# A recurrence followed by a gated feed-forward on one core: one down projection stands at another place, and the last tile is stored differently

## The chip, the cores and the metric

The kernel runs on one core of one Trainium2 chip. The number that counts is device time of one execution in microseconds (us). Before the change it is 585.62 us, the median of three runs (585.18 to 587.04 us).

## The reference

Two stages follow each other. The first is a linear recurrence over 768 steps for 4 batches of 8 heads with 48 channels each; the second takes its output as 3072 tokens of 384 values and applies a gated feed-forward with 1536 inner units.

```python
for t in range(S):
    kt, vt, rt = (k[:, :, t], v[:, :, t], r[:, :, t])
    cur = np.einsum('bhd,bhe->bhde', u[None] * kt, vt)
    y[:, :, t] = np.einsum('bhd,bhde->bhe', rt, state + cur)
    state = w[None, :, :, None] * state + np.einsum('bhd,bhe->bhde', kt, vt)

gate = 1.0 / (1.0 + np.exp(-(x @ w_gate)))
val = x @ w_val
return (gate * val @ w_out).astype(np.float32)
```

## The kernel before

**Tiling.** The 768 steps are cut into 12 chunks of 64. The heads of a chunk form two groups, so there are 24 groups, numbered 0 to 23. Two chunks make a tile of 512 tokens, and the feed-forward works through six tiles (0 to 5) in 12 slices of 128 inner units each.

**One slice of the feed-forward** is: 18 matmuls of 128x512 into two PSUM banks (`up`, L443), a sigmoid on ACT (L452), a product on DVE (L456), a rounding to fp32r on ACT (L461), the remainder on POOL or DVE (L465), and 9 matmuls (`down`, L481) that add to three accumulator banks, acc0 to acc2. Operands are kept as a rounded part and a remainder, and three products are formed of them. The down projection of a slice stands one slice late, so that its inputs are ready. After slice 11 of a tile the three banks are written out by `store` (L490): for each bank ACT copies the left 256 columns (L493), DVE the right 256 (L494), both into one `wf` buffer, of which there are two, and SP issues one DMA of 256 KB to the result.

**One group of the recurrence** is: `scores` (L304; for groups from 8 on it begins with the 32 matmuls that read the state, L284, then 64 matmuls into `sc`, L315), `keep` (L320, two masked copies on DVE, L323), `apply` (32 matmuls `ring<-score,toks`, L284, then in `outer` 32 matmuls `ring<-toks`), `x_high` (ACT, L402) and `x_low` (DVE, L406), which write the next feed-forward tile's input, and `add_state` (DVE, L379), which releases the PSUM bank that the next `up` needs. `prepare` (ACT L259, POOL L265 and L275, DVE L271) readies the next group, and `load` (SP, L101 and L106) fetches one further on.

**What sets the order.** Every engine executes its instructions in the order in which the program records them. The first part (tile 0 with groups 0 to 7) is written out as a table of steps (`START`, L42): the letter names the step and the number its group or slice; `U` is `up`, `g m H q` are the parts after it, `D` is `finish` (a down projection, with the store after the last one), `L X` are loads and `A R k T` are the four parts of `prepare`. From item 13 on (slice 0 of tile 1) a loop (L563) records for each item: `up`, the gate, then for slices 0, 3, 6 and 9 the scores and the masked copies of one group, then the down projection of the item before, then the rest of the group. Items are counted through: 0 to 12 belong to tile 0 (its first slice has two halves), 13 to 24 to tile 1, and so on. In the loop, `finish(i - 1)` is left out for item 13, because the table has already recorded `D.12`.

After the loop there is a branch (L597) around a fallback for unusual decays; it is not taken into the fallback here.

Of the kernel before, what the change touches and what calls it, by code (L numbers as in the profile page):

```python
# [10 lines left out]
F32 = mybir.dt.float32  # L11
# [7 lines left out]
B, H, S, D = 4, 8, 768, 48  # L19
DM, DF = H * D, 1536  # L20
P = 128
# [4 lines left out]
CT = B * C  # L26
# [7 lines left out]
TILES = [[c, c + 1] for c in range(0, NC, 2)]  # L34
# [15 lines left out]
U.4 Tv.6 j.6 Z.6 g.4 ov.5 w.6 D.3 m.4 c.7 o.6 K.6 H.4 U.5 j.7 c.8 g.5 qv.4 w.7 j.8 I.6 O.6 h.6 D.4  # L50
d.6 m.5 w.8 l.6 s.6 F.6 H.5 ov.7 U.6 qv.5 c.9 ov.8 k.7 c.10 Tv.7 j.9 Z.7 g.6 D.5 m.6 U.7 w.9 K.7
H.6 o.9 j.10 g.7 q.6 c.11 I.7 O.7 h.7 D.6 d.7 m.7 l.7 H.7 s.7 F.7 w.10 q.7 j.11 U.8 ov.10 D.7 w.11
g.8 ov.11 U.9 m.8 H.8 q.8 D.8 g.9 m.9 H.9 L.8 X.8 U.10 q.9 D.9 g.10 m.10 H.10 U.11 q.10 D.10 g.11
m.11 H.11 U.12 q.11 A.8 R.8 k.8 T.8 D.11 g.12 m.12 H.12 qv.12 D.12
"""


# [1 line left out]
def rwkv_then_moe(ctx: ExitStack, tc: tile.TileContext, wd, ch, tk, wt, rk0, vn0, wd0, out):  # L59
    nc = tc.nc  # L60
# [3 lines left out]
    hp = ctx.enter_context(tc.tile_pool(name="hp", bufs=2))  # L64
    hq = ctx.enter_context(tc.tile_pool(name="hq", bufs=2))
    wtmp = ctx.enter_context(tc.tile_pool(name="wtmp", bufs=2))
# [136 lines left out]
    W3, WH = 3 * DM, 3 * DM // 2  # L203
# [100 lines left out]
    def scores(n):  # L304
        t, r, k = dec[n], chan[n][:, 0], chan[n][:, 1]
        sc = ga[n] = two_banks()
        if n >= FIRST:
            yb[n] = one_bank(), one_bank()
            from_state(n)
        for kk, rr, at in ((k, t[:, 0], 0), (t[:, 1], r, 256)):  # L310
            for p, p2 in PP:
                o = at + (2 * p + p2) * C
                for be, gm in QUARTERS:
                    row, cs = slice(64 * be, 64 * be + D), (4 * p + 2 * (be ^ gm) + p2) * C
                    nc.tensor.matmul(  # L315
                        sc[64 * gm : 64 * gm + 64, be, o : o + C],
                        kk[row, cs : cs + C], rr[row, cs : cs + C], start=True, stop=True,
                    )

    def keep(n):  # L320
        sc, t = ga.pop(n), score[n % 2]
        for m, at in ((0, 0), (1, 256)):
            nc.vector.copy_predicated(  # L323
                t.rearrange("q (b m i) -> q b m i", b=2, m=4),
                masks[:, m].bitcast(I32).unsqueeze(1).unsqueeze(1).broadcast_to([P, 2, 4, C]),
                sc[:, :, at : at + 256].rearrange("q b (m i) -> q b m i", m=4),
            )

    def apply(n):
        c, g = GROUPS[n]  # L330
        v, t = toks[n][:, 1], score[n % 2]
        if n < FIRST:
            yb[n] = one_bank(), one_bank()
            if c:
                from_state(n)
                nc.tensor.drain()
        for p, p2 in PP:
            for s in range(2):
                for gm in range(2):
                    be, row = gm ^ s, slice(64 * gm, 64 * gm + 64)  # L340
                    m, at = D if s else 64, (4 * p + 2 * be + p2) * D
                    i = (4 * be + 2 * p + p2) * C
                    into_y(
                        n, s, be, m, slice((2 * p + p2) * C, (2 * p + p2 + 1) * C),
                        v[row, at : at + m], t[row, i : i + C], True,
                    )

    def outer(n):
        k, v = toks[n][:, 0], toks[n][:, 1]
        for p, p2 in PP:  # L350
            for be in range(2):
                for gm in range(2):
                    row, at = slice(64 * gm, 64 * gm + 64), (4 * p + 2 * be + p2) * D
                    m, o = D if be else 64, 256 + (2 * p + p2) * D
                    into_y(
                        n, be, gm ^ be, m, slice(o, o + D), k[row, at : at + m],
                        v[row, at : at + D], True,
                    )
# [6 lines left out]
    def decay_state(n):  # L365
        g, st = states(n)
        for p in range(2):
            for s in range(2):
                nc.scalar.activation(  # L369
                    st[:, p, s], st[:, p, s], AF.Copy,  # L370
                    scale=pw[0:112, 4 * g + 2 * p + s, 64:65],
                )

    def add_state(n):
        g, st = states(n)
        for s in range(2):
            y = yb[n][s][0:112, 256 : 256 + 4 * D].rearrange("q (p x) -> q p x", p=2)
            if GROUPS[n][0]:
                nc.vector.tensor_tensor(st[:, :, s], st[:, :, s], y, ALU.add)  # L379
            else:  # L380
                nc.vector.tensor_copy(st[:, :, s], y)
# [18 lines left out]
    def x_high(n):  # L400
        for x, y in x_of(n, 0):
            nc.scalar.copy(out=x, in_=y)  # L402

    def x_low(n):
        for (x, y), (hi, _) in zip(x_of(n, 1), x_of(n, 0)):
            nc.vector.tensor_tensor(x, y, hi, ALU.subtract)  # L406
# [8 lines left out]
    def fills(n):  # L415
        c, g = GROUPS[n]
        ti = TILE_OF[c]
        if ti == 0:
            co = CT * TILES[ti].index(c)
            for j in range(3) if g == 1 else ():  # L420
                fill(xt[ti], j, slice(co, co + CT))
        elif c == TILES[ti][-1]:
            for j in (2,) if g == 1 else (0, 1):
                fill(xt[ti], j, slice(0, 2 * CT))
# [62 lines left out]
    def accumulators():  # L487
        return [pacc.tile([P, 512], F32, name=f"acc{d}") for d in range(3)]

    def store(acc, dst):  # L490
        for d in range(3):
            o = wtmp.tile([P, W3], F32, name="wf")[:, 0:512]
            nc.scalar.copy(out=o[:, 0:CT], in_=acc[d][:, 0:CT])  # L493
            nc.vector.tensor_copy(o[:, CT:], acc[d][:, CT:])  # L494
            nc.sync.dma_start(
                out=out[d * P : (d + 1) * P, dst], in_=o.rearrange("q (c t) -> q c t", t=CT)
            )


    halves = [(0, g) for g in range(HALF)] + [(1, g) for g in range(HALF)] + [(2, g) for g in range(HALF, NF)]  # L500
    items = [(0, h, f) for h, f in halves]
    n0 = len(items)
    for ti in range(1, len(TILES)):
        items += [(ti, 2, f) for f in range(NF)]
    moes, accs = {}, {}

    def moe_of(it):
        ti, h, f = it
        if ti not in accs:
            accs[ti] = accumulators()  # L510
        if (ti, h) not in moes:
            cols = (slice(0, CT), slice(CT, 2 * CT), slice(0, 2 * CT))[h]
            moes[ti, h] = Moe(xt[ti], accs[ti], cols)
        return moes[ti, h]

    def finish(i):
        ti, h, f = items[i]
        moe_of(items[i]).down(f)
        if f == NF - 1:
            store(accs[ti], slice(TILES[ti][0], TILES[ti][-1] + 1))  # L520


    steps = {
# [19 lines left out]
    for step in START.split():  # L543
        name, _, arg = step.partition(".")
# [3 lines left out]
    def prepare(n):  # L548
        if n < len(GROUPS):
            bonus_keys(n)  # L550
            queries(n)
            keys(n)
            if GROUPS[n][0] < NC - 1:
                token_keys(n)

    def load(n):
        if n < len(GROUPS):
            load_channels(n)
            load_tokens(n)
# [3 lines left out]
    for i in range(n0, len(items)):  # L563
        ti, h, f = items[i]
        m = moe_of(items[i])
        m.up(f)
        m.gate(f)
        attend = f in SLOTS and n < 4 * (ti + 2) and n < len(GROUPS)
        if attend:
            scores(n)  # L570
            if GROUPS[n][0] < NC - 1:
                decay_state(n)
            keep(n)
        if i > n0:
            finish(i - 1)
        if attend:
            apply(n)
            if GROUPS[n][0] < NC - 1:
                outer(n)
            x_high(n)  # L580
            x_low(n)
            if GROUPS[n][0] < NC - 1:
                add_state(n)
            prepare(n + 1)
            fills(n)
            load(n + 2)
            n += 1
        if i == n0 + 8:
            range_flag()
    assert n == len(GROUPS)  # L590
    finish(len(items) - 1)


# [3 lines left out]
    with tc.If(bad != 0):  # L597
        with ExitStack() as g:
# [22 lines left out]
            with tc.For_i(0, NC) as c:  # L621
                for p in range(NP):
                    nc.sync.dma_start(
                        out=rkc[:, p].rearrange("q a b i -> q (a b i)"),
                        in_=rk0[bass.ds(c, 1), p].rearrange("o q x -> (o q) x"),
                    )
                with tc.For_i(0, C) as i:
                    for lo, side in ((0, 1), (64, 0)):
# [3 lines left out]
                        for p in range(NP):  # L632
                            nc.sync.dma_start(
                                out=vb[lo : lo + D, p], in_=src[:, p].broadcast_to([D, B, 64])
# [25 lines left out]
                    out=xg[bass.ds(c, 1)].rearrange("o q p t -> (o q) p t"),  # L660
                    in_=yc.rearrange("q p b i -> q p (b i)"),
# [3 lines left out]
            with tc.For_i(0, NC, 2) as c:  # L665
                for j in range(3):
                    for to, lo, n, p in (
# [3 lines left out]
                            out=xr[to : to + n, j],  # L671
                            in_=xg[bass.ds(c, 2), lo : lo + n, p].rearrange("c q t -> q c t"),
# [4 lines left out]
                m = Moe(x, accumulators(), slice(0, 512))  # L677
# [93 lines left out]
```

## Time and profile before

| | before |
|---|---|
| median of the runs | 585.62 us |
| the profiled execution's own time | 585.8 us |
| its span | 584.0 us |
| PE (matmul) busy | 539.5 us, 92% |
| DVE, ACT, POOL busy | 36%, 33%, 25% |

The span is the time from the first to the last instruction of the program on the core; about 1.8 us of the execution's time lie around it. PE is busy for 92% of the span, the other compute engines for about a third, and matmul records overlap a little, because a matmul's record reaches to the end of its pipeline. In a timeline a group of equal instructions on one engine is one row with its start, its length, and in square brackets the idle time before it with what ended it. A suffix q (SPq) is the engine's sequencer, which issues DMAs.

### The profile page before, as it was taken

The page shows a single profiled execution, that of the slowest core. Times are in us where ns is not written, and L with a number is a line of the kernel's source. Part 1 is how long each engine was busy: PE and PEld are TensorE (multiplying, and loading weights), DVE is VectorE, ACT ScalarE, POOL GpSimd, SP SyncE. Part 2 cuts the span into 40 slices and gives each one's busy share as a digit, 9 for nine tenths or more (in the row PEclk, how much of TensorE's full clock was granted, in tenths as well). Part 3 has the DMA queues.
Part 4 walks back from the last instruction along what each step waited for, and adds up shares of the span by engine and source line. Part 5 has one row for each costly group of instructions (what it writes and reads, how often), then busy time and mean ns, then how long its engine had stood idle before and what let it go on. Part 6 is the DMA issues. An engine that isn't in the chain of part 4 may idle for free. (4 is left out here: it accounts for less than half of the span.)

```text
span 584.0 us, 12860 instructions
## 1 busy us (share of the span) xinstructions
PE 539.5 (92%) x5689; PEld 435.8 (75%) x5689; DVE 212.5 (36%) x339; ACT 190.0 (33%) x421; POOL 147.2 (25%) x125
## 2 busy tenths in 40 slices
PE   3755988999899999999999999999999999999994
PEld 2645866788688878788888778878778788888882
DVE  7787999932313313312312313312313212101101
ACT  4365565432323313413313413313413212211221
POOL 3420410322213313313313313313312211211210
PEclk9966998999799999999999999999999999999998
DMA  8489440110600112230012130023130001100001
GB/s 310 176 345 353 153 183 10 33 52 18 231 2 1 15 60 84 62 122 2 9 67 83 59 126 2 7 68 84 57 128 2 9 3 19 55 1 1 0 0 59
DMA packets 13117, 44.54 MB, mean 76 GB/s; under 512 B 2080, under 2 KB 2464, under 8 KB 11648
## 3 DMA queue, kind: packets, MB, share of 16 engines
q1 hardware_dynamic: 13056, 43.66, 21.9%
q8 instruction: 46, 0.75, 0.5%
q14 instruction: 15, 0.12, 0.1%
HBM read 36.58 MB, written 4.72 MB: 71 GB/s over the span
## 5 line engine op out<-in xcount | busy, mean ns | idle before, releaser
L443 PE MATMUL ring<-xt,wx 128*128 128x512 f32 (+1 forms) x1314 | 323.2, 400 | 12.8 <-DVE wf L224 7.2
L443 PEld LDWEIGHTS ring<-xt,wx 128*128 128x128 f32 x1314 | 248.2, 193 | 71.8 <-issue 9.3
L465 POOL TENSOR_TENSOR h<-sg,h 128x512 fp32r<-128x512 f32 x68 | 89.6, 1318 | 363.9 <-ACT h L461 363.9
L481 PE MATMUL acc<-h,wx 128*128 128x512 f32 (+1 forms) x657 | 163.0, 392 | 0.4 <-POOLq L597 0.4
L456 DVE TENSOR_TENSOR sg<-ring,sg 128x512 f32<-128x512 f32 (+1 forms) x73 | 49.9, 684 | 287.9 <-PE ring L443 287.9
L481 PEld LDWEIGHTS acc<-h,wx 128*128 128x128 f32 x657 | 120.5, 188 | 27.7 <-POOLq L597 0.8
L461 ACT CAST h<-sg 128x512 fp32r<-128x512 f32 (+1 forms) x73 | 44.8, 614 | 146.5 <-DVE sg L456 146.5
L452 ACT ACTIVATE sg<-ring 128x512 f32<-128x512 f32 (+1 forms) x73 | 43.2, 592 | 143.6 <-PE ring L443 143.5
L323 DVE COPY_PREDICATED score<-masks,sc 128x512 f32<-128x512 int32 x48 | 36.0, 751 | 14.7 <-PE sc L315 13.9
L265 POOL TENSOR_TENSOR dec<-chan,tabk 128x512 f32<-128x512 f32 x21 | 29.1, 1385 | 20.6 <-DMA chan<-in_ch 12.7
L402 ACT CAST xt<-ring 112x256 fp32r<-112x256 f32 (+1 forms) x52 | 17.2, 375 | 45.5 <-PE ring L284 45.4
L259 ACT ACTIVATE dec<-chan,wu 128x128 f32<-128x128 f32 x96 | 30.7, 399 | 2.9 <-DMA chan<-in_ch 2.9
L406 DVE TENSOR_TENSOR xt<-ring,xt 112x256 fp32r<-112x256 f32 (+1 forms) x52 | 19.9, 419 | 30.2 <-ACT xt L402 28.7
L315 PE MATMUL sc<-dec,chan 48*64 48x64 f32 x768 | 17.4, 232 | 8.5 <-DVE chan L271 7.2
L284 PEld LDWEIGHTS ring<-score,toks 64*48 64x48 f32 (+1 forms) x768 | 15.4, 143 | 12.3 <-issue 6.9
L284 PEld LDWEIGHTS ring<-dec,state 48*48 48x48 f32 (+1 forms) x704 | 13.6, 134 | 13.8 <-issue 8.3
L284 PE MATMUL ring<-score,toks 64*48 64x64 f32 (+1 forms) x768 | 18.8, 242 | 5.4 <-DVE score L323 4.0
L369 ACT ACTIVATE state<-state,pw 112x96 f32<-112x96 f32 x80 | 23.4, 366 | 0.0
L284 PE MATMUL ring<-dec,state 48*48 48x64 f32 (+1 forms) x704 | 17.1, 230 | 6.3 <-ACT sg L452 4.5
L315 PEld LDWEIGHTS sc<-dec,chan 48*64 48x64 f32 x768 | 14.9, 146 | 10.3 <-DVE chan L271 7.2
L275 POOL TENSOR_TENSOR toks<-toks,tabn 128x384 f32<-128x384 f32 x17 | 18.0, 1060 | 9.6 <-ACT tabn L181 8.7
L216 ACT ACTIVATE wf<-wr 128x1152 f32<-128x1152 f32 (+1 forms) x13 | 15.3, 1192 | 15.3 <-DMA wr<-in_wt 10.7
(48 smaller groups left out, 213.9 us busy)
## 6 DMA issues: line engine op xcount, KB each, us to landing
wr<-in_wt SPq DMA_DIRECT2D x11, 1152.0 KB, 8.7
chan<-in_ch SPq DMA_DIRECT2D x24, 512.0 KB, 4.1
toks<-in_tk SPq DMA_DIRECT2D x24, 400.0 KB, 4.7
out_y<-wf SPq DMA_DIRECT2D x18, 256.0 KB, 2.2
xt<-xt SPq DMA_DIRECT2D x30, 64.0 KB, 2.3
wr<-in_wt SPq DMA_DIRECT2D x2, 576.0 KB, 7.2
xt<-xt SPq DMA_DIRECT2D x12, 32.0 KB, 4.8
wu<-in_wd SPq DMA_DIRECT2D x1, 8.0 KB, 1.6
```

What stands on the lines that cost most here:

```text
L259: nc.scalar.activation(t[:, 1, cs], k[:, cs], AF.Copy, scale=wu[:, 1, 4 * g + m : 4 * g + m + 1])
L265: eng.tensor_tensor(v4(t[:, 0]), v4(chan[n][:, 0]), bc2(table_of(n)[:, :, ::-1]), ALU.mult)
L284: nc.tensor.matmul(yb[n][bank][64 * half : 64 * half + m, cs], lhsT, rhs, start=first, stop=stop, skip_group_check=True,)
L315: nc.tensor.matmul(sc[64 * gm : 64 * gm + 64, be, o : o + C], kk[row, cs : cs + C], rr[row, cs : cs + C], start=True, stop=True,)
L323: nc.vector.copy_predicated(t.rearrange("q (b m i) -> q b m i", b=2, m=4), masks[:, m].bitcast(I32).unsqueeze(1).unsqueeze(1).broadcast_to ...
L369: nc.scalar.activation(st[:, p, s], st[:, p, s], AF.Copy, scale=pw[0:112, 4 * g + 2 * p + s, 64:65],)
L443: nc.tensor.matmul(o[:, self.cols], w[a][:, g * DM + kt * P : g * DM + (kt + 1) * P], self.x[:, kt, b, self.cols], start=(k == 0), stop=(k ...
L452: nc.scalar.activation(sg[:, c], self.pair[f][0][:, c], AF.Sigmoid)
L456: nc.vector.tensor_tensor(sg[:, c], self.pair.pop(f)[1][:, c], sg[:, c], ALU.mult)
L461: nc.scalar.copy(out=h[:, 0, c], in_=sg[:, c])
L465: eng.tensor_tensor(h[:, 1, c], self.sg.pop(f)[:, c], h[:, 0, c], ALU.subtract)
L481: nc.tensor.matmul(self.acc[d][:, self.cols], w[a][:, 2 * DM + d * P : 2 * DM + (d + 1) * P], h[:, b, self.cols], start=(f == 0 and k == 0 ...
```

## The change

Two edits in the order and one in the store.

- `D.12`, the last down projection of tile 0 with the store of that tile, leaves the end of the table. The loop now calls `finish(i - 1)` for item 13 too, so it stands behind the scores and masked copies of group 8 and ahead of that group's `apply`.
- `A.8 R.8 k.8 T.8` (the preparation of group 8) stand one slice earlier in the table, ahead of `D.10`.
- The last tile is written out by a new function, `store_last`. Bank 0 is copied whole by ACT and bank 1 whole by DVE, each into a `wf` buffer. Bank 2 is copied in two halves, one by ACT and one by DVE, into two `sg` buffers, and each half has a DMA of its own. So there are four DMAs instead of three, and none of the copies takes a buffer from which an earlier bank is still being sent.

```diff
-g.8 ov.11 U.9 m.8 H.8 q.8 D.8 g.9 m.9 H.9 L.8 X.8 U.10 q.9 D.9 g.10 m.10 H.10 U.11 q.10 D.10 g.11
-m.11 H.11 U.12 q.11 A.8 R.8 k.8 T.8 D.11 g.12 m.12 H.12 qv.12 D.12
+g.8 ov.11 U.9 m.8 H.8 q.8 D.8 g.9 m.9 H.9 L.8 X.8 U.10 q.9 D.9 g.10 m.10 H.10 U.11 q.10 A.8 R.8
+k.8 T.8 D.10 g.11 m.11 H.11 U.12 q.11 D.11 g.12 m.12 H.12 qv.12
...
+    def store_last(acc, c):
+        copies = nc.scalar.copy, nc.vector.tensor_copy
+        for d in range(2):
+            o = wtmp.tile([P, W3], F32, name="wf")[:, 0:512]
+            copies[d](out=o, in_=acc[d])
+            nc.sync.dma_start(
+                out=out[d * P : (d + 1) * P, c : c + 2], in_=o.rearrange("q (c t) -> q c t", t=CT)
+            )
+        for i in range(2):
+            o = hp.tile([P, 512], F32, name="sg")[:, 0:CT]
+            copies[i](out=o, in_=acc[2][:, i * CT : (i + 1) * CT])
+            nc.sync.dma_start(out=out[2 * P : 3 * P, c + i], in_=o)
...
         if f == NF - 1:
-            store(accs[ti], slice(TILES[ti][0], TILES[ti][-1] + 1))
+            if ti == len(TILES) - 1:
+                store_last(accs[ti], TILES[ti][0])
+            else:
+                store(accs[ti], slice(TILES[ti][0], TILES[ti][-1] + 1))
...
-        if i > n0:
-            finish(i - 1)
+        finish(i - 1)
```

On PE, around the start of tile 1, before the change. The accumulators of tile 0 are `acc_416` to `acc_418`; `L315` are the last matmuls of the scores of group 8, and `ring<-score_98,toks` begins its `apply`:

```order
L481 MATMUL acc_416<-h,wx 128x512 x3
L481 MATMUL acc_417<-h,wx 128x512 x3
L481 MATMUL acc_418<-h,wx 128x512 x3
L443 MATMUL ring<-xt,wx 128x512 x18
...
L315 MATMUL sc<-dec,chan 64x64 x16
L315 MATMUL sc<-chan,dec 64x64 x16
L284 MATMUL ring<-score_98,toks 64x64 x2
```

The same place on PE with the change:

```order
L443 MATMUL ring<-xt,wx 128x512 x18
...
L315 MATMUL sc<-dec,chan 64x64 x16
L315 MATMUL sc<-chan,dec 64x64 x16
L481 MATMUL acc_416<-h,wx 128x512 x3
L481 MATMUL acc_417<-h,wx 128x512 x3
L481 MATMUL acc_418<-h,wx 128x512 x3
L284 MATMUL ring<-score_98,toks 64x64 x2
```

The nine matmuls have moved past one `up` and the scores, and now stand between the scores and the `apply` of group 8.

On SP, the DMA issues from the loads of group 8 to those of group 10, before and with the change (minus and plus):

```order
 L101 DMA chan<-in_ch 128x1024
 L106 DMA toks<-in_tk 128x800
-L495 DMA out_y<-wf 128x512 x3
 L101 DMA chan<-in_ch 128x1024
 L106 DMA toks<-in_tk 128x800
+L495 DMA out_y<-wf 128x512 x3
 L101 DMA chan<-in_ch 128x1024
 L106 DMA toks<-in_tk 128x800
```

The loads of group 9 have moved ahead of the three stores of tile 0; those of group 10 still follow them.

On DVE, the copies that `store_last` makes at the end of the program and what each waits for, with the change (`acc_5014` and `acc_5015` are banks 1 and 2 of the last tile; the words in brackets are the engines and DMAs waited for):

```order
L456 TENSOR_TENSOR sg<-ring,sg 128x512 [waits PE_49,Activation_49] x11
L504 COPY wf<-acc_5014 128x512 [waits DMAHW6_49,PE_49]
L510 COPY sg<-acc_5015 128x256 [waits Activation_49,Pool_49]
L612 TENSOR_LOAD flag [waits DVE_49]
L613 COMPARE_AND_BRANCH
```

DVE has two copies there instead of three; the first waits for PE and no longer for ACT, the second waits for ACT.

## Rows read from the trace of the kernel before

**Rows 1.** Page, part 1: busy us, share of the span, instructions.

```profile
PE 539.5 (92%) x5689; PEld 435.8 (75%) x5689; DVE 212.5 (36%) x339; ACT 190.0 (33%) x421; POOL 147.2 (25%) x125
```

**Rows 2.** Timeline of PE, 140 to 164: start, length, what, [idle before, releaser].

```profile
140.63 4.28 PE L481 MATMUL acc<-h,wx 128*128 128x512 f32 x18
144.75 4.36 PE L443 MATMUL ring<-xt,wx 128*128 128x512 f32 x18
149.04 0.68 PE L284 MATMUL ring<-dec,state 48*64 48x64 f32 x32
...
152.29 1.12 PE L284 MATMUL ring<-score,toks 64*64 64x64 f32 x32 [1.64 <-DVE score L323]
...
154.74 0.46 PE L284 MATMUL ring<-toks 64*48 64x48 f32 x9 [0.72 <-issue]
155.13 6.22 PE L443 MATMUL ring<-xt,wx 128*128 128x512 f32 x18
161.19 2.25 PE L481 MATMUL acc<-h,wx 128*128 128x512 f32 x9
```

**Rows 3.** Windows: stretch, its length, busy us (count) of PE, PEld, DVE, ACT, POOL, clock, DMA.

```profile
152.20:159.00 6.80, 5.99 (x73) 4.96 (x74) 2.01 (x6) 1.81 (x6) 2.27 (x2) 0.50 0.81 301
239.40:249.30 9.90, 9.50 (x189) 7.55 (x189) 5.24 (x11) 4.97 (x15) 3.50 (x3) 1.00 0.39 122
```

**Rows 4.** Timeline, 239 to 250: the start of tile 2 on PE and ACT.

```profile
239.48 0.68 PE L284 MATMUL ring<-dec,state 48*64 48x64 f32 x32
...
245.20 0.38 ACT L493 COPY wf<-acc 128x256 f32<-128x256 f32 x1 [2.12 <-DMA out_y<-wf]
...
247.10 2.33 PE L443 MATMUL ring<-xt,wx 128*128 128x512 f32 x9 [0.40 <-DVE state L379]
...
249.27 2.25 PE L481 MATMUL acc<-h,wx 128*128 128x512 f32 x9
```

**Rows 5.** Timeline of PE, 320 to 340: the start of tile 3.

```profile
327.25 0.68 PE L284 MATMUL ring<-dec,state 48*64 48x64 f32 x32
...
337.29 2.21 PE L481 MATMUL acc<-h,wx 128*128 128x512 f32 x9
```

**Rows 6.** Timeline of ACT and SP, 114 to 134.

```profile
114.45 0.53 SPq L101 DMA_DIRECT2D chan<-in_ch  x1
...
132.55 0.60 ACT L452 ACTIVATE sg<-ring 128x512 f32<-128x512 f32 x1 [2.79 <-PE ring L443]
```

**Rows 7.** Windows, columns as in Rows 3: one slice earlier, and where group 8 is prepared.

```profile
129.90:135.90 6.00, 6.00 (x28) 4.86 (x27) 0.69 (x1) 1.11 (x2) 1.24 (x1) 1.00 0.00 0
135.90:140.40 4.50, 4.50 (x21) 3.62 (x20) 0.71 (x1) 1.89 (x6) 3.97 (x3) 1.00 0.00 0
```

**Rows 8.** Timeline, 573 to 579: the last tile's copies and DMA issues.

```profile
574.29 0.37 ACT L493 COPY wf<-acc 128x256 f32<-128x256 f32 x1 [1.95 <-PE acc L481]
574.70 0.42 DVE L494 COPY wf<-acc 128x256 f32<-128x256 f32 x1 [3.01 <-ACT wf L493]
574.98 0.37 ACT L493 COPY wf<-acc 128x256 f32<-128x256 f32 x1 [0.32 <-PE acc L481]
...
575.84 0.90 SPq L495 DMA_DIRECT2D out_y<-wf  x1
...
577.93 0.37 ACT L493 COPY wf<-acc 128x256 f32<-128x256 f32 x1 [2.57 <-PEq L597]
...
578.79 0.33 SPq L495 DMA_DIRECT2D out_y<-wf  x1
```

**Rows 9.** Source line L597, the branch: durations ns min/median/max, first and last start.

```profile
L597 SPq EVENT_SEMAPHORE  x8: 17/17/17, 582.1 to 582.6; - x8
...
L597 SPq COMPARE_BRANCH  x1: 45/45/45, 579.2 to 579.2; - x1
```

**Rows 10.** DMA issues, 148 to 156 and 575 to 577: count, KB, median us to landing.

```profile
chan<-in_ch SPq DMA_DIRECT2D x3, 512.0 KB, 6.6
...
out_y<-wf SPq DMA_DIRECT2D x2, 256.0 KB, 2.6
```

## The prediction

> **What bounds the kernel now.** I read the shares of the page first: PE is busy for 92% of the span [rows 1], so time can be won only where PE stands still or runs slowly, or behind its last matmul. Then the timeline of PE around the two places that the change touches, then the granted clock in windows, and last the timeline and the branch at the end.
>
> At the start of tile 1 the reader is to see a hole. The down projections of items 11 and 12 run back to back from 140.63, `up` of item 13 from 144.75, the state and score matmuls of group 8 from 149.04; then PE waits 1.64 us for the masked copies of DVE and later 0.72 us more, until `up` of item 14 begins at 155.13 and takes until 161.19 [rows 2]. The masked copies cannot begin before the scores end, and nothing stands between the scores and `apply` on PE. Over 152.2 to 159.0 the granted clock is 0.50, the lower of the two levels (1.2 GHz) [rows 3]; before it PE had run the small matmuls of the scores and then stood still. So `up` of item 14 takes 155.13 to 161.19 = 6.06 us, where item 13's takes 144.75 to 149.04 = 4.29.
>
> The starts of tiles 2 and 3 already have the order that tile 1 is to get: scores, down projection with its store, apply. There the whole chain from the state matmuls to the next down projection takes 249.27 - 239.48 = 9.79 us at a clock of 1.00 [rows 3, 4] and 337.29 - 327.25 = 10.04 us [rows 5].
>
> At the end the third bank waits. Banks 0 and 1 are copied from 574.29 and 574.98, but the third copy starts only at 577.93, when the first bank's DMA has landed and its `wf` buffer is free (the view names PE's sequencer there; but PE's last matmul is long done. DVE ends the first bank at 574.70 + 0.42 = 575.12, the issue follows 0.03 later, and the DMAs land 2.6 us after issue: 575.15 + 2.6 = 577.75). Its DMA is issued at 578.79 [rows 8, 10]. SP then branches at 579.2, and its next instruction stands at 582.1 [rows 9], from where a fixed chain leads to the end at 584.0.
>
> **Part 1, the moved down projection.** Its 9 matmuls cost the same, 4.12 / 2 = 2.06 us by the start-to-start of the eighteen [rows 2]. New times: item 11's down ends at 140.63 + 2.06 = 142.69; `up` of item 13 takes 4.29, so the state matmuls of group 8 begin at 146.98; from there the rows of tiles 2 and 3 stand for what comes, 9.79 to 10.04, I take 9.9. The next down projection begins at 156.9 instead of 161.19: **4.3 us won**, 4.15 to 4.4 by the two rows. The two idle times (2.36 us) and the slow `up` (1.77 us) are the larger part of it; the rest is the apply that no longer runs at the lower clock.
>
> What the move adds is in the 9.79 to 10.04 already: the three copies of ACT and DVE now stand ahead of `x_high` and `add_state` of group 8 on those engines, and the third one waits for a landed DMA (2.12 us at tile 2), which shows on PE as 0.40 us before the second half of the next `up` [rows 4, 5]. The input of the moved matmuls is ready well before they now begin, at about 148.5, since before the change they ran from 142.69. On SP the loads of group 9 pass the three stores. They can be issued right behind those of group 8 at 114.45 [rows 6], when group 6, whose buffers they take, is done; so the stores do not run against them, and the preparation of group 9 does not wait for a load. That costs nothing: SP only has to wait for buffers that are free by then, and if they are not, the last rival below is the price.
>
> **Part 2, the preparation of group 8, one slice earlier.** Four ACT, one DVE and two POOL instructions. Where they stand before, ACT is busy for 1.89, DVE 0.71 and POOL 3.97 us in a window of 4.5, other work included; in the 6.0 us one slice earlier they are busy for 1.11, 0.69 and 1.24 [rows 7]. The two together fit into the 6.0 on each engine (3.0, 1.4 and 5.2). ACT has one hole for it, 2.79 us ahead of the sigmoid at 132.55 [rows 6], and gets no more than 1.89. PE is busy throughout both windows. Cost: **0**; the cover is 0.9 us on ACT (2.79 less 1.89), and beyond that the sigmoid would be late by the rest. The loads that it needs are issued from 114.45 on.
>
> **Part 3, the last store.** Bank 0: one ACT copy of 512 columns instead of 256; ACT takes 0.60 us for 512 columns out of PSUM [rows 6]. 574.29 + 0.60 = 574.89, and SP issues at 574.92 (the step from a copy's end to SP's issue is 0.03 us at the third bank: 577.93 + 0.37, 0.04 to DVE, + 0.42 gives 578.76, and SP issues at 578.79). Bank 1: DVE needs 0.69 for 512 columns [rows 7], from 574.98 to 575.67; issue 575.70. Bank 2 is complete 0.69 us after bank 1, the distance of the first two copies, at 575.67. ACT's half takes 0.37, to 576.04; DVE's half waits for ACT's and takes 0.42, from 576.07 to 576.49 [rows 8].
>
> Could the halves run side by side? DVE's copy of a half starts at 574.70, behind the end of ACT's at 574.66 [rows 8]; before the change both also write one buffer, with the change they don't, but DVE's wait for ACT is still listed. The sum takes them one after the other. The Trainium skill, "PSUM — Partial Sum Buffer", section "PSUM bank collisions raise a hardware error", has two engines that read one bank at the same time as an error, so by that rule the split of bank 2 can't earn an overlap; side by side, DVE would be done 0.4 us sooner, of which SP's issues below would let through less than 0.1. The trace agrees with the rule, with 0.04 us between the two.
>
> SP's second issue took 0.90 us, from 575.84 to 576.74, where the last one took 0.33 [rows 8]. I take it that whatever held it until 576.74 is still there, because PE's end has not moved. Then the third issue runs 576.79 to 577.12 and the fourth 577.17 to 577.50, and SP branches at 577.54 instead of 579.16 (578.79 + 0.33 and the same step): **1.6 us won**. If the hold is gone, DVE's half sets the fourth issue, 576.53 to 576.86, and 2.3 us are won. The fourth DMA lands by 577.17 + 2.6 = 579.8, before SP's next instruction at 577.54 + 2.9 = 580.4 (579.2 to 582.1 in [rows 9]), so the landing does not set the end. The other bound: if the end did go by the landing and a half lands no sooner than a whole bank, the win is 578.79 - 577.17 = 1.6 again.
>
> **Sum.** 4.3 + 1.6 = 5.9 us off the profiled execution's 585.8 (span 584.0 and 1.8 around it) gives 579.9; the median of the runs lies 0.2 lower, so **579.7 us**.
>
> **Rivals.**
> - *The clock falls all the same.* The small matmuls of scores and apply are still there, and the pause before the second half of `up` comes on top. Price: 1.77 for `up` and about half of the 152.29 to 155.13 stretch without its idle time, 1.06, together 2.8: 582.5. Against it: the window of tile 2 has the same sequence and a clock of 1.00 [rows 3]. The Trainium skill, "TensorE: Matmul & The Clock Gate", section "HAM oscillation — how this bites in real kernels", speaks for it: it puts such a fall down to idle gaps longer than any single one here, so by that rule alone closing the hole would not bring the clock back. The trace doesn't settle what else was in play at 152, but it does show the sequence that is to come at the upper level.
> - *The end is set elsewhere.* If another engine or a late landing sets it, part 3 earns nothing: 581.3. Against it: the end before follows SP's instruction at 582.1 [rows 9], and PE, ACT and DVE all end no later than now.
> - *The move does not close the hole.* If `apply` waits for something else than the masked copies, the down projection only changes places with idle time that reappears: part 1 gives 0, 584.0. Against it: the wait is put down to DVE's L323, and at tile 2 the same L323 is passed with no such wait in the 9.79 us [rows 2, 4].
> - *Slower: the stores land late.* The loads of group 9 now stand ahead of the stores on SP. If their buffers came free only with the scores of group 8, they would be issued just ahead of the stores, which would land like crowded loads, 6.6 us after issue instead of 2.6 [rows 10]. ACT's third copy, `x_high`, `add_state` and the next `up` would wait 4.0 us longer and the clock would fall, 2.8: 579.7 + 6.8 = 586.5. It decides from a delay of about 3 us on, with the clock lost as well. Against it: SP issued the loads of group 8 from 114.45 on [rows 6], and the buffers that group 9 takes are those of a group two before it.
>
> **How the numbers follow.** The forecast has 0.74, with a range of its own of 579.0 to 580.2 (0.65 us for the hold on SP's issue, 0.25 for the two tile starts); the clock 0.08; the end set elsewhere 0.09; the hole that stays 0.05; late stores 0.04. The range 578.8 to 581.5 holds the forecast and the end set elsewhere, 0.83 together. What can be told from no change is 0.3%, 1.8 us: faster means below 583.9. The first three cases are faster, 0.91, and 0.02 of the fourth, where the end wins 2.3 (583.3), so 0.93; the rest of the fourth and a milder case of late stores are the same, 0.04; slower 0.03.
>
> **What would show it.** In the changed profile: the 9 matmuls of L481 between L315 and L284 at about 148.5, no wait of L284 for L323, clock 1.00 through the stretch, a wait of ACT for `out_y<-wf` at about 152.5 and a PE pause of 0.4 to 0.7 for L379; the next down projection at 156.8 to 157.0, and everything until the last tile 4.2 to 4.4 earlier. At the end, with times less that shift: four issues, the last at about 577.2, no copy that waits for a DMA, and SP's branch to its next instruction again 2.9. A clock of 0.50 behind 150, a pause over 1 us at L379, or an SP gap that has grown would each make it wrong.

## The result, and the profile after

The changed kernel takes 579.99 us (median of 6 runs, 577.57 to 581.18), the kernel before 585.69 us in the same comparison (6 runs, 582.72 to 587.04). The ratio is 0.9901 with a 95% interval of 0.9872 to 0.9931: 5.7 us faster, where 579.7 and 5.9 were forecast. The profiled execution took 580.07 us, its span fell from 584.0 to 578.3. In the experiments below one run each of e4 and e6 was slow (756 and 764 us, at a granted clock of 0.66 and 0.65) and is left out of their medians.

First the timeline of the start of tile 1 on PE in the changed kernel, the answer to [rows 2]. Columns are start, length, what, and the idle time before with its releaser.

```profile
140.49 2.22 PE L481 MATMUL acc<-h,wx 128*128 128x512 f32 x9
142.54 4.36 PE L443 MATMUL ring<-xt,wx 128*128 128x512 f32 x18
146.83 0.68 PE L284 MATMUL ring<-dec,state 48*64 48x64 f32 x32
...
148.38 2.32 PE L481 MATMUL acc<-h,wx 128*128 128x512 f32 x9
150.63 0.68 PE L284 MATMUL ring<-score,toks 64*64 64x64 f32 x32
151.12 0.64 PE L284 MATMUL ring<-toks 64*48 64x48 f32 x32
151.69 2.36 PE L443 MATMUL ring<-xt,wx 128*128 128x512 f32 x9
154.51 2.33 PE L443 MATMUL ring<-xt,wx 128*128 128x512 f32 x9 [0.46 <-DVE state L379]
156.68 2.21 PE L481 MATMUL acc<-h,wx 128*128 128x512 f32 x9
```

And the copy that now waits there on ACT, the answer to the ACT row of [rows 4]:

```profile
152.61 0.37 ACT L493 COPY wf<-acc 128x256 f32<-128x256 f32 x1 [2.18 <-DMA out_y<-wf]
```

The nine matmuls stand at 148.38, between the scores and `apply`; the wait for the masked copies is gone, and so is the second pause. What is left is 0.46 us before the second half of `up`. The next down projection begins at 156.68. Counted from item 11's down projection, that is 16.19 us instead of 161.19 - 140.63 = 20.56: **4.37 us won here**, 4.3 forecast.

The granted clock of the same stretch, the answer to [rows 3] (stretch, length, busy us and count of PE, PEld, DVE, ACT, POOL, clock, DMA share, GB/s):

```profile
152.00:159.00 7.00, 6.54 (x29) 5.05 (x28) 2.99 (x7) 3.20 (x9) 0.63 (x1) 1.00 0.78 247
```

The clock is 1.00, the upper level (2.4 GHz), where it was 0.50.

Then the end, the answer to [rows 8]: the last tile's copies on ACT and DVE, in the timeline of the changed kernel.

```profile
569.16 1.88 PE L481 MATMUL acc<-h,wx 128*128 128x512 f32 x7 [0.36 <-POOLq L613]
569.70 0.59 ACT L504 COPY wf<-acc 128x512 f32<-128x512 f32 x1 [1.95 <-PE acc L481]
570.40 0.69 DVE L504 COPY wf<-acc 128x512 f32<-128x512 f32 x1 [3.30 <-PE acc L481]
571.13 0.37 ACT L510 COPY sg<-acc 128x256 f32<-128x256 f32 x1 [0.85 <-PE acc L481]
571.61 0.42 DVE L510 COPY sg<-acc 128x256 f32<-128x256 f32 x1 [0.52 <-ACT sg L510]
```

SP's four issues, one by one:

```profile
570.31 0.33 SPq L505 DMA_DIRECT2D out_y<-wf  x1
571.12 1.22 SPq L505 DMA_DIRECT2D out_y<-wf  x1
572.46 0.35 SPq L511 DMA_DIRECT2D out_y<-sg  x1
572.91 0.93 SPq L511 DMA_DIRECT2D out_y<-sg  x1
```

Shifted by the 4.59 us derived below, the copies start as forecast to within 0.13 us: bank 0 in 0.59, bank 1 in 0.69, the two halves of bank 2 one after the other, and none waits for a DMA. But two of the four issues are held on SP, the second for 1.22 and the fourth for 0.93 us. And the branch, the answer to [rows 9], by line (durations in ns, first and last start):

```profile
L613 SPq EVENT_SEMAPHORE  x8: 17/17/17, 576.4 to 576.9; - x8
...
L613 SPq COMPARE_BRANCH  x1: 45/45/45, 573.9 to 573.9; - x1
```

The last down projection has moved from 573.75, where the kernel before resumes it, to 569.16, by 4.59; the end has moved by 5.72 (584.02 to 578.30). From the start of the last matmul to the end it is 8.77 us before and 7.64 now. So the end itself is worth **1.1 us**, where 1.6 was forecast. The two stretches make 5.5 us; of the 0.2 us that are left of the 5.72, 0.14 had passed before the first thing that the change moves on PE (item 11's down projection begins at 140.63 before and 140.49 now).

Single runs of one kernel scatter by up to 7 us (e2: 580.74 to 587.64). The traces show one source of it: the start of item 11's down projection, 140 us into the program and ahead of everything the change touches but the earlier preparation, lies between 139.87 and 142.54 in the ten traces used here. So effects of one microsecond are read below from stretches between two instructions of one trace, and the medians serve as the check. That the median came within 0.3 us of the forecast is in part luck: at this scatter it could have missed by more with the same mechanism.

### The profile page after: what moved, and what is told of

Read it like the earlier page. It is cut to its first block, busy times and chain, and to the rows that moved or that the text cites. A ratio compares the mean times of both kernels' runs of the same rounds, so it can differ in the third digit from the quotient of the medians.

```text
span 578.3 us, 12857 instructions
## 1 busy us (share of the span) xinstructions
PE 534.4 (92%) x5689; PEld 431.4 (75%) x5689; DVE 211.7 (37%) x338; ACT 189.4 (33%) x420; POOL 146.1 (25%) x125
## 5 line engine op out<-in xcount | busy, mean ns | idle before, releaser
L443 PE MATMUL ring<-xt,wx 128*128 128x512 f32 (+1 forms) x1314 | 319.8, 396 | 14.2 <-DMA xt<-xt 7.6
L443 PEld LDWEIGHTS ring<-xt,wx 128*128 128x128 f32 x1314 | 245.4, 191 | 72.6 <-issue 9.7
L456 DVE TENSOR_TENSOR sg<-ring,sg 128x512 f32<-128x512 f32 (+1 forms) x73 | 49.9, 684 | 289.4 <-PE ring L443 289.4
L315 PE MATMUL sc<-dec,chan 48*64 48x64 f32 x768 | 17.2, 231 | 9.8 <-DVE chan L271 7.3
L315 PEld LDWEIGHTS sc<-dec,chan 48*64 48x64 f32 x768 | 14.8, 145 | 11.6 <-DVE chan L271 7.3
```

The costliest lines, as they stand in the source:

```text
L315: nc.tensor.matmul(sc[64 * gm : 64 * gm + 64, be, o : o + C], kk[row, cs : cs + C], rr[row, cs : cs + C], start=True, stop=True,)
L443: nc.tensor.matmul(o[:, self.cols], w[a][:, g * DM + kt * P : g * DM + (kt + 1) * P], self.x[:, kt, b, self.cols], start=(k == 0), stop=(k ...
L456: nc.vector.tensor_tensor(sg[:, c], self.pair.pop(f)[1][:, c], sg[:, c], ALU.mult)
```

## The experiments

Theory: the order wins 4.4 us by closing one hole and keeping the clock up, the store wins about one by not waiting for a landed DMA. Rivals: the win is at the end; it is the place of the down projection or its store that matters, not the hole; it is the loads that passed the stores; the earlier preparation does it. All runs are compared with the kernel before on the same chip: 585.39 us (25 runs) for e1 to e4, 586.18 (17 runs) for e5, e6, e8 and e9.

**e1, the order alone.** The last tile is stored as before.

```diff
-            if ti == len(TILES) - 1:
-                store_last(accs[ti], TILES[ti][0])
-            else:
-                store(accs[ti], slice(TILES[ti][0], TILES[ti][-1] + 1))
+            store(accs[ti], slice(TILES[ti][0], TILES[ti][-1] + 1))
```

> Parts 1 and 2 alone: the order of the change, the last tile's store as before. If the hole at the start of tile 1 and the lower clock behind it are what the order removes, the down projection of item 13 begins at 156.5 to 157.0 instead of 161.2, the clock is 1.00 throughout, and the time is 4.3 to 4.6 us under the kernel before, about 581.2; the last tile's copies still wait for a landed DMA. If most of the 5.7 us came from the end, the time is within 2 us of the kernel before.

581.17 us (8 runs), ratio 0.9928 (0.9900 to 0.9955): 4.2 us faster. The next down projection begins at 156.37, 16.39 us after item 11's, and the clock is 1.00. As expected: about three quarters of the win are the order's.

**e2, the store alone.** The table and the loop are those of before.

```diff
-        finish(i - 1)
+        if i > n0:
+            finish(i - 1)
```

> Part 3 alone: the order as before, the last tile stored by the new function. By the traces the end is shorter by 1.1 us (as measured with the whole change) to 1.6 us (as predicted), so about 584.4; hole and clock of 0.50 at 152 stay. If the end were set by something else than SP's issues, it is the time of the kernel before.

583.70 us (12 runs), ratio 0.9971 (0.9947 to 0.9996): 1.7 us faster. From the start of PE's last matmul to the end it takes 8.04 us; the kernel before and e1 take 8.77 and 9.09, the changed kernel 7.64. So the store is worth 0.7 to 1.5 us by these traces; the median's 1.7 has an interval of 0.2 to 3.1. All ten traces agree: the stretch takes 8.77 to 9.29 us with the old store (before, e1, e4, e8) and 7.22 to 8.34 with the four DMAs (the change, e2, e3, e6). The hole is still there, and its second pause is longer than before. PE, timeline of e2:

```profile
154.20 0.68 PE L284 MATMUL ring<-score,toks 64*64 64x64 f32 x32 [1.64 <-DVE score L323]
154.70 0.52 PE L284 MATMUL ring<-toks 64*48 64x48 f32 x23
156.85 0.46 PE L284 MATMUL ring<-toks 64*48 64x48 f32 x9 [1.63 <-issue]
157.24 6.64 PE L443 MATMUL ring<-xt,wx 128*128 128x512 f32 x18
```

The first wait is the same 1.64 to the hundredth, the second 1.63 instead of 0.72, and `up` again runs slowly. The apply itself runs at the upper level here (0.68 us, before the change 1.12).

**e3, without the earlier preparation.** `A.8 R.8 k.8 T.8` back in their place.

```diff
-U.10 q.9 D.9 g.10 m.10 H.10 U.11 q.10 A.8 R.8 k.8 T.8 D.10 g.11 m.11 H.11 U.12 q.11 D.11
+U.10 q.9 D.9 g.10 m.10 H.10 U.11 q.10 D.10 g.11 m.11 H.11 U.12 q.11 A.8 R.8 k.8 T.8 D.11
```

> The whole change without part 2: the preparation of group 8 stands where it stood before. If part 2 costs and brings nothing, the time is that of the whole change, about 580.0, and the scores of group 8 begin within 0.2 us of its 146.8. If the earlier preparation is what lets the scores and the sigmoid of items 12 and 13 run in time, PE shows a wait of 0.5 us or more between 135 and 150.

580.32 us (6 runs), ratio 0.9910 (0.9880 to 0.9939), against 0.9901 for the whole change. From item 11's down projection to item 13's it takes 156.20 - 140.01 = 16.19, the same to the hundredth, and PE has no pause between 135 and 150. The scores begin at 146.36 and not within 0.2 us of 146.8, but item 11's down projection stands 0.48 us earlier too. Part 2 costs and brings nothing that can be seen. At its end this run shows something else, to which I come back: eight instructions of SP behind the branch.

```profile
L613 SPq EVENT_SEMAPHORE  x8: 17/17/17, 575.9 to 577.1; - x8
```

They take 1.2 us where the changed kernel's take 0.5.

**e4, other work in the hole.** The kernel before; the down projection of item 12 and its store stay in the table. The first half of item 14's `up` goes between scores and apply, item 13's down projection ahead of the second half.

```diff
-        def up(self, f):
+        def up(self, f, halves=range(2)):
...
-            for g in range(2):
+            for g in halves:
...
-        m.up(f)
+        m.up(f, (1,) if i == n0 + 1 else (0, 1))
...
-        if i > n0:
+        if i > n0 + 1:
             finish(i - 1)
+        if i == n0:
+            m.up(f + 1, (0,))
         if attend:
             apply(n)
             if GROUPS[n][0] < NC - 1:
                 outer(n)
+            if i == n0:
+                finish(i)
```

> The kernel before with the hole filled by other work: the down projection of item 12 and its store stay where they were, and the first half of the up of item 14 (9 matmuls) stands between the scores and the apply of group 8, the down projection of item 13 between the apply and the second half of that up. If the hole is what costs (idle time and the clock behind it), the clock stays at 1.00 and 4.2 to 5.0 us are won, as with the order alone: about 581. If it is the place of the down projection or of its store that matters, the clock falls to 0.50 all the same and less than 2.5 us (the idle time) are won.

581.99 us (11 runs), ratio 0.9943 (0.9921 to 0.9966): 3.4 us faster. PE, timeline of e4:

```profile
151.56 2.36 PE L443 MATMUL ring<-xt,wx 128*128 128x512 f32 x9
153.85 0.68 PE L284 MATMUL ring<-score,toks 64*64 64x64 f32 x32
154.35 0.40 PE L284 MATMUL ring<-toks 64*48 64x48 f32 x14
155.75 0.44 PE L284 MATMUL ring<-toks 64*48 64x48 f32 x18 [0.99 <-issue]
156.12 2.33 PE L481 MATMUL acc<-h,wx 128*128 128x512 f32 x9
158.29 6.46 PE L443 MATMUL ring<-xt,wx 128*128 128x512 f32 x27
```

The 27 matmuls at 158.29 take 6.46 us, the rate of the upper level, and the window agrees (columns as above):

```profile
155.00:165.00 10.00, 9.25 (x56) 7.55 (x56) 2.81 (x7) 3.53 (x9) 2.28 (x2) 1.00 0.35 129
```

The wait for the masked copies is gone with the down projection and the store in their old place, and the clock stays up through the pause of 0.99 us that is left. From item 11's down projection to item 14's it takes 164.58 - 141.59 = 22.99 us; the kernel before takes 26.84, the changed one 22.42. So it need not be this down projection and its store that fill the hole; other long work brings most of the win. The expectation was 4.2 to 5.0; 3.85 in the trace is less, by less than the 0.99 us of the pause that I had not counted on.

**e8, the loads early.** The kernel before, with the loads of group 9 in front of the stores on SP.

```diff
-... g.9 m.9 H.9 L.8 X.8 U.10 ...
+... g.9 m.9 H.9 L.8 X.8 L.9 X.9 U.10 ...
...
-    load(n + 1)
```

> The kernel before, with the loads of group 9 ahead of the down projection and stores of tile 0 on SP, as the change has them; nothing else. If the loads that crowd in behind the stores are what makes PE stop in the outer of group 8 (0.72 us for no semaphore, 1.6 with the new store alone), that pause goes; the wait of 1.64 us for the masked copies stays. If the clock falls for the 1.64 us alone, 0.5 to 1.5 us are won, about 584.5; if it takes both pauses to make it fall, the clock stays at 1.00 and 3.3 to 4 us are won, about 581.8.

586.19 us (12 runs), ratio 1.0000 (0.9981 to 1.0019). The pause did not go, so neither case of the expectation came. SP in the timeline of e8, the load of group 9, the stores of tile 0, and the loads behind them:

```profile
114.87 0.37 SPq L101 DMA_DIRECT2D chan<-in_ch  x1
...
143.73 3.55 SPq L495 DMA_DIRECT2D out_y<-wf  x3
147.38 0.42 SPq L101 DMA_DIRECT2D chan<-in_ch  x1
147.90 0.41 SPq L106 DMA_DIRECT2D toks<-in_tk  x1
150.06 0.33 SPq L101 DMA_DIRECT2D chan<-in_ch  x1
```

PE, timeline of e8:

```profile
151.59 0.68 PE L284 MATMUL ring<-score,toks 64*64 64x64 f32 x32 [1.64 <-DVE score L323]
152.08 0.52 PE L284 MATMUL ring<-toks 64*48 64x48 f32 x23
154.35 0.46 PE L284 MATMUL ring<-toks 64*48 64x48 f32 x9 [1.74 <-issue]
```

The loads of group 9 are issued 29 us before the stores, and the second pause is still there, longer. But the crowd of loads is still there too: SP now issues the next ones right behind the stores, so this run doesn't take it away. It does show that the new place of group 9's loads alone wins nothing. What the pause is can be read from the traces. In every kernel that has it one 16 KB block of instructions is being fetched just ahead of it (queue q8 of the DMA table; before the change 46 such packets with 0.75 MB; PE holds most of the program's instructions, so I take the block for PE's), and PE goes on a nearly fixed time after that block's end. The columns are: when the state matmuls of group 8 begin, when the block is fetched, what all DMAs move between these two, when the pause ends, and how far behind the fetch.

| | state matmuls | fetch of the block | moved in between | pause ends | behind the fetch |
|---|---|---|---|---|---|
| before | 149.04 | 152.41 to 153.41 | 268 GB/s | 154.74 | 1.33 |
| e2 | 150.94 | 154.55 to 155.57 | 273 GB/s | 156.85 | 1.28 |
| e4 | 150.02 | 153.43 to 154.39 | 273 GB/s | 155.75 | 1.36 |
| e8 | 148.34 | 151.96 to 152.96 | 300 GB/s | 154.35 | 1.39 |
| the change | 146.83 | 147.88 to 148.96 | 0 GB/s | no pause | |

The place in PE's stream fits as well: in e4 nine more matmuls stand ahead of the `outer`, and the pause comes after 14 of its matmuls instead of 23. In the changed kernel the fetch begins 1.05 us behind the state matmuls instead of 3.4 to 3.6, the block is there before the nine long matmuls of the down projection are done, and PE doesn't pause; in e1, e3, e5, e6 and e9, which have the new order too, it is 1.0 to 1.7 us. It is not PE's wait for the masked copies that makes the fetch late, since e4 doesn't have that wait. What goes with the late fetch in all ten traces is the traffic: with the old place of the stores they and the loads behind them are under way in that stretch, with the new order at most 16 GB/s are. That the fetch queues behind them is not shown, since no run takes that traffic alone away.

The scores, the apply and the outer are 160 matmuls that go by quickly (32 of them take 151.12 - 150.63 = 0.49 us from start to start in the changed kernel, some 15 ns each); where they reach a block that has not come yet, PE stands until it is there. The Trainium skill, "Runtime: NRT & Kernel Launch", section "Instruction fetch mechanics", describes these blocks and calls their cost mostly hidden; here it was 0.7 to 1.7 us.

**e5, three DMAs at the end.** The change, with both halves of bank 2 in one `sg` buffer and one DMA.

```diff
+        o = hp.tile([P, 512], F32, name="sg")
         for i in range(2):
-            o = hp.tile([P, 512], F32, name="sg")[:, 0:CT]
-            copies[i](out=o, in_=acc[2][:, i * CT : (i + 1) * CT])
-            nc.sync.dma_start(out=out[2 * P : 3 * P, c + i], in_=o)
+            cs = slice(i * CT, (i + 1) * CT)
+            copies[i](out=o[:, cs], in_=acc[2][:, cs])
+        nc.sync.dma_start(out=out[2 * P : 3 * P, c : c + 2], in_=o.rearrange("q (c t) -> q c t", t=CT))
```

> The whole change, with the two halves of bank 2 in one buffer and sent by one DMA of 256 KB instead of two of 128 KB. If SP's row of held issues sets the end, SP branches about 1 us earlier after the last matmul (2.2 instead of 3.2 us after its start) and the end stands 0.7 to 1.5 us closer to it (about 6.9 us after its start, where the whole change has 7.64): about 579.2. If the landing of the last bytes sets it, or two halves land sooner than a whole, the end is as far from the last matmul as with the whole change, 7.6 to 8.3, or farther.

579.62 us (6 runs), ratio 0.9901 (0.9872 to 0.9931), the whole change's own ratio. In the trace the end stands 6.88 us behind the start of the last matmul, as expected, 0.76 closer than with four DMAs; by the medians it is 0.4 us, too little to be told from nothing. e9, which has three DMAs too, takes 6.94 us there, so both lie under the 7.22 to 8.34 of the four traces with four DMAs. SP's last issue in the timeline of e5:

```profile
571.71 0.62 SPq L512 DMA_DIRECT2D out_y<-sg  x1
```

And its branch, by line:

```profile
L614 SPq EVENT_SEMAPHORE  x8: 17/17/17, 575.3 to 575.9; - x8
...
L614 SPq COMPARE_BRANCH  x1: 45/45/45, 572.4 to 572.4; - x1
```

SP branches 2.0 us after the start of the last matmul (570.37) instead of 3.2 (573.88 and 570.65), because there is one issue less; the time from the branch to its next instruction is again 2.9.

**e6, no copy waits, in any tile.** The change, and in `store` too the third bank goes into an `sg` buffer.

```diff
-            o = wtmp.tile([P, W3], F32, name="wf")[:, 0:512]
+            o = wtmp.tile([P, W3], F32, name="wf")[:, 0:512] if d < 2 else hp.tile([P, 512], F32, name="sg")
```

> The whole change, and in the other tiles too the third bank is copied into an sg buffer, so that no copy waits for a landed DMA. If that wait is what delays x_high and add_state and so the second half of the up at a tile's start, the pauses of 0.39 to 0.68 us for L379 at the starts of tiles 1 to 4 go, 1.5 to 2.0 us in all: about 578.2. If those pauses come from x_high, x_low and add_state themselves, they stay and the time is that of the whole change.

577.36 us (5 runs), ratio 0.9873 (0.9842 to 0.9905). Timeline of e6 at the start of tile 1:

```profile
151.11 0.37 ACT L493 COPY sg<-acc 128x256 f32<-128x256 f32 x1 [0.36 <-PE acc L481]
...
152.01 4.44 PE L443 MATMUL ring<-xt,wx 128*128 128x512 f32 x18
...
153.24 0.61 DVE L379 TENSOR_TENSOR state<-state,ring 112x192 f32<-112x192 f32 x2
...
156.29 2.01 PE L481 MATMUL acc<-h,wx 128*128 128x512 f32 x8
```

ACT's third copy waits for PE alone, DVE's `add_state` starts 1.23 us behind the start of `up` (in the changed kernel 2.33), and `up` runs through in 4.28 us from start to start, where the changed kernel takes 156.68 - 151.69 = 4.99. PE's pauses for L379 are gone at the starts of all four tiles; in the changed kernel they were 0.46, 0.39, 0.68 and 0.45, 1.98 in all. From item 11's down projection to the last matmul it takes 427.4 us, in the changed kernel 430.2: 2.8 us, more than the pauses, as a row's idle time counts only from the end of the last matmul's record. The median is 2.6 lower; by the ratios it is 1.6, with intervals that overlap.

**e9, both.** The edits of e5 and e6 on top of the change.

> The two edits of e5 and e6 together on top of the change. If both hold, their gains add: 1.5 to 2.0 us at the tile starts and 0.7 to 1.5 at the end, about 577.2, under both kernels. If one falls, it is as fast as the other alone.

576.57 us (5 runs), ratio 0.9847 (0.9818 to 0.9875): 9.6 us under the kernel before and 3.4 under the changed one, the fastest of all. From item 11's down projection to the end of the trace it takes 434.3 us, e6 434.6, e5 437.4 and the changed kernel 437.8. So both gains are in it; that they add is clear for e6's, while e5's is too small here to be told from the scatter of the ends.

## Why the prediction was right, point by point

**Part 1** was right in its size and for its main reason. The chain of tiles 2 and 3 [rows 4, 5] stood for what tile 1 would become, and it did: from the state matmuls to the next down projection 156.68 - 146.83 = 9.85 us, between the 9.79 and 10.04 of the rows. The first wait, the clock and the new pause came as described. e1 shows that the order alone does it, e4 that other long work in the hole brings most of it.

One reason was not given. The second pause was counted as part of the hole and taken to vanish with it; its cause was left open. By the traces it is a wait for PE's own instructions, and it vanishes because their block is fetched about 2 us earlier with the new order, not because the masked copies are waited for no more: in e4 the first wait is gone, nine long matmuls stand in its place, and this pause is there. It was also not a fixed 0.72: 1.63 and 1.74 in e2 and e8. What sets it is when the block has come. So the apply at the lower clock, to which the prediction gives the rest of the win, cost nothing by itself: from its start to the end of the pause it is 2.45 us before the change, and 2.65 and 2.76 in e2 and e8, where the apply ran at the upper level.

**The clock.** The rival that it falls all the same is out: 1.00 in the changed kernel, in e1 and in e4, and the rule that the prediction puts behind this rival is not borne out here. With the wait of 1.64 us it fell in all three traces (before, e2, e8), without it in none of the seven others, which have the same small matmuls ahead. The second pause isn't needed for it: before the change the clock is already down 1.8 us before that pause begins; in e2 it falls as that pause begins and in e8 0.36 us into it. The window of the kernel before, columns as above:

```profile
152.20:154.00 1.80, 1.71 (x55) 1.57 (x56) 0.04 (x1) 0.00 (x0) 1.27 (x1) 0.50 1.03 406
```

But a wait of PE doesn't bring it down each time. Some 47 us before item 11's down projection, ahead of everything that the change moves, PE waits 1.96 to 1.99 us for a product of DVE (L456) in all ten traces; behind that wait the clock falls to 0.50 in three (before, e1, e4) and stays at 1.00 in seven. What decides there isn't shown, nor whether the clock falls at the hole in every execution of the kernel before.

**Part 2** was right at 0 (e3). That the loads on SP pass the stores was costed at nothing, and nothing can be seen of it (e8, ratio 1.0000).

**Part 3** was right in its mechanism and too large: 1.6 forecast, 1.1 in the trace. The copies came as worked out. Three terms did not. The second issue, taken as held until a fixed time, ended 0.18 later than that. The fourth issue was taken at 0.33 us and took 0.93. With 0.15 more in the steps between the issues SP branched at 573.88 instead of 572.95 (577.54 less the shift of 4.59): of the 1.6 us 0.7 were left. And the time from the branch to SP's next instruction was 2.5 instead of 2.9, which gave 0.4 back. The step that failed is "the fourth 577.17 to 577.50". The trace shows what is new there: ACT and DVE reach their own branches at 571.9 and 572.3, since they no longer wait for a DMA, and an 8 KB block of instructions (queue q14) is fetched from 572.96 to 573.71, a microsecond behind ACT's branch and in the middle of SP's fourth issue, which ends 0.13 behind it. The hold on the second issue, which the prediction tied to PE's end, fits the same way: it ends 0.37 behind a 16 KB block (q8) whose fetch begins just behind the start of the last matmul, before the change as with it (576.37 and 576.74, 571.97 and 572.33). The twelve held store issues at the ends of nine traces all end so, nine of them 0.37 to 0.39 behind a 16 KB block and three 0.13 or 0.14 behind an 8 KB one; e5's third with its 0.62 us is one of them. A fetch alone isn't enough: the third issue of the kernel before took 0.33 in the middle of one (578.50 to 579.44), when no earlier store was under way. So this is what fits, not what is shown.

"The landing does not set the end" held by a hair. The DMAs land 2.8 to 3.8 us after issue here, not 2.6, the last at 576.55, when SP's first instruction behind the branch had already begun at 576.4. In e2 and e3 SP does wait for the last one: its eight instructions take 0.9 (583.6 to 584.5) and 1.2 us instead of 0.5. So with four DMAs the branch and the landing are now about equally late. With one issue and its bytes gone the end is closer, 6.88 us in e5 and 6.94 in e9 instead of 7.64; the medians can't confirm that.

**The rivals.** That the stores land late did not happen: the ACT row shows a wait of 2.18 us for a landed DMA, like tile 2's 2.12. But it was the place to look at: that wait is the one that e6 removes, and it brings 2.8 us over four tiles by the traces.

## What to carry to other kernels

A hole in the bounding engine costs more than its length: here 1.6 us of waiting stood beside a clock that fell and a code fetch that came late, 4.4 us in all, and two kinds of long work put into it each won most of that back. When a new order exists elsewhere in the same program, its own rows there are the best forecast, with all its new waits in them. At the end of a program count the issues on the queue that finishes last, one by one: here some were held for up to a microsecond, and splitting a transfer adds one.

## What the runs showed of the hardware that was not expected

- PE can run out of instructions in a stretch of small matmuls: 0.72, 0.99, 1.63 and 1.74 us, each ending 1.28 to 1.39 us behind the fetch of a 16 KB block, and in each of these four traces that fetch began 3.4 to 3.6 us behind the state matmuls of group 8, while 268 to 300 GB/s moved; in the six others it began 1.0 to 1.7 us behind them, at 16 GB/s or less, and PE had no such pause.
- The clock fell with a wait of 1.64 us at the hole in three of three traces, and with a wait of 1.96 to 1.99 us at another place in three of ten.
- A store's issue on SP that mostly takes 0.33 us took 0.62 to 1.37 at the ends of nine traces where instructions were being fetched beside it and an earlier store was under way, and 0.33 in e4, where the fetch began 0.02 us after the issue.
- From a taken branch to SP's next instruction 2.5 to 3.1 us pass, whether its DMAs have landed (before, e5) or not (the change, e2, e3).
